# Identity products on TensorE ahead of the first keys, and an earlier place for two norms

## The chip, the cores and the metric

The kernel runs on one core of a Trainium2 chip. A time is the device time of one execution in microseconds (us); the time of the kernel is the median of several executions. Engines are named as the profile names them: PE is TensorE (PEld its weight loads), DVE is VectorE, ACT is ScalarE, POOL is GpSimd, SP is SyncE, which issues most of the DMAs.

## The reference

Two layers. The first is a linear attention with a complex decay, for 4 sequences of 768 steps, 8 heads of 48:

```python
mag = np.sqrt(a_re * a_re + a_im * a_im)
scale = np.minimum(mag, 0.999) / (mag + 1e-06)
a_re_n, a_im_n = (a_re * scale, a_im * scale)
for t in range(S):                       # S = 768
    new_re = ar * S_re - ai * S_im       # ar, ai: the decay of step t
    new_im = ar * S_im + ai * S_re
    kv = np.einsum('bhd,bhe->bhde', k[:, :, t], v[:, :, t])
    S_re, S_im = (new_re + kv, new_im)
    y[:, :, t] = np.einsum('bhd,bhde->bhe', q[:, :, t], S_re)
```

The second takes its 3072 rows of 384 through 8 experts, all of them dense, weighted by a matrix that 8 rounds of row and column scaling make of the gate's logits:

```python
P = np.exp(logits)                       # 3072 x 8
for _ in range(8):
    P /= P.sum(1, keepdims=True) + 1e-09
    P /= P.sum(0, keepdims=True) + 1e-09
    P *= N / E
for e in range(E):                       # E = 8, F = 1024
    out += P[:, e:e + 1] * (np.maximum(x @ w1[e], 0.0) @ w2[e])
```

## The kernel before

The 3072 rows are cut into 12 blocks of 256 (`SUB`), each of two chunks of 128. In the first phase (`phase1`) a block goes through these stations:

- **norm** (`chain`, first half; L450 to L464): the magnitude of the decay is brought to 0.999 at most. ACT squares `z` (the decays) into `sq` (L450), DVE adds (`x`, L455), ACT takes the root twice (`y`, `zz`, L456 to L457), DVE and ACT refine it (L458 to L462), and DVE scales `z` (L464). Blocks 0 to 2 (`NHALF` = 3) do this in two halves, one for each chunk; later blocks in one piece of 768 columns.
- **scan** (`scan`, `cmul`; L368 to L373): DVE forms the running complex products of the decays along a chunk in many small operations on `z` with the temporaries `cm_a` and `cm_b`.
- **keys and queries** (`chain`, second half; L472 to L487): from the products ACT and DVE make the scaled keys `kh` (L485) and, in place of `z`, the scaled queries (L487). The last operation on the queries of block i, half n, is kept as `zl[i, n]`, the second root on ACT (L478) as `sqs[i, n]`. For blocks in one piece n is 0.
- **mix** (`mix`): DMAs spread `kh` into `ks` (SP's queue) and `z` into `qs` (POOL's queue), L510. PE transposes the keys (`ktp`, L531), which ACT copies (`kt`, L533), forms the scores (`sp`, L548), which DVE masks into `sc` (L551), the new state (`U`, L541), which DVE adds up (L602 to L613), and the outputs (`y`, L565). ACT and DVE split them into a rounded part `xh` (L617) and the rest `xl` (L618).
- **experts 0 and 1** (`experts`): 16 steps for a block, 8 for each expert. A step is nine products of `xh` and `xl` with a piece of the first weights (`ph`, L215), two passes on ACT (`hh`, `hf`, L227 and L228), the rest `hl` on DVE (L229), and, up to three steps later (`LAG`), the products with the second weights (`po`, L188 to L190). A block's steps stand between the pieces of the next block's mix.

The second phase takes the other six experts through products that share sums; it is PE's work from end to end and holds most of the time.

Ahead of the mix of block 0, PE also splits the weights. A weight is needed as a rounded part and a rest; `load_w` and `thirds` make the rest on PE, as the identity times the raw weight less the identity times the rounded part (`wd`, L138 and L139 for whole pieces, L164 and L165 for thirds), and ACT copies it out of PSUM (L143, L167). There are two PSUM buffers for each of the two kinds of `wd`, so a piece on PE waits for a copy on ACT. The copies of expert 1 are put behind `g1`, the second root of block 0's second half, on ACT.

The order of the work is set in two ways. PE runs in the order in which the program is written (a manual schedule). For DVE, ACT, POOL and SP a list scheduler orders the instructions by a time line that it works out itself when the program is built. `tc.issue_after(x)` tells it not to put an instruction ahead of `x`. In `chain` this holds the norm of a block behind an operation of the block before:

```python
prev = {2: (1, NCH - 1), 3: (2, NCH - 1), 4: (3, 0)}.get(i)
```

ACT's first square is behind `sqs[prev]`, DVE's first operation behind `zl[prev]`. For blocks 0 to 2 there are fixed orders on DVE and ACT besides. Line numbers are those of the kernel before.

Of the kernel before, what the change touches and what calls it, by code (L numbers as in the profile page):

```python
# [6 lines left out]
F32 = mybir.dt.float32  # L7
# [8 lines left out]
NCT = C // 128  # L16
E, F = 8, 1024
NF = F // 128
CH = 128
SUB = 256  # L20
NCH = SUB // CH
# [2 lines left out]
N1 = 8  # L24
RING = 12
LAG = 3
NHALF = 3
LEAD = {1: 12, 2: 10, 3: 9, 4: 7, 5: 5}
TR = 4
# [6 lines left out]
HEAD = 3  # L36
# [25 lines left out]
class Net:  # L62
# [63 lines left out]
    def load_w(self, e, f, wx, late=None, pool=False):  # L126
        nc = self.nc
        t = self.wt[e, f] = self.wp.tile([128, 2, 2 * C], F32R, tag="w", name=f"w{e}_{f}")
        raw = wx.tile([128, 2 * C], F32, tag="w", name=f"wr{e}_{f}")
        self.wl = nc.sync.dma_start(raw, self.w[e, f])  # L130
        if not pool:
            nc.scalar.activation(t[:, 0, :], raw, AF.Copy)
        else:
            nc.gpsimd.tensor_copy(t[:, 0, :], raw)
        for j in range(2):
            cs = slice(j * C, j * C + C)
            d = (self.psB if j else self.psA).tile([128, C], F32, tag="po" if j else "ph", name=f"wd{e}_{f}_{j}")
            nc.tensor.matmul(d, self.ident, raw[:, cs], start=True, stop=False)  # L138
            nc.tensor.matmul(d, self.nident, t[:, 0, cs], start=False, stop=True)  # L139
            with ExitStack() as st:  # L140
                if late is not None:
                    st.enter_context(self.tc.issue_after(late.ins))
                self.ev.append(nc.scalar.activation(t[:, 1, cs], d, AF.Copy))  # L143

    def thirds(self, e, fs, wx, late):
        nc = self.nc
# [2 lines left out]
        def one(t, f, j):  # L149
# [4 lines left out]
            self.nthird += 1  # L154
            mid = HEAD <= n < 2 * (LAG + 1)
            if not mid:
# [20 lines left out]
    def experts(self):  # L177
# [18 lines left out]
        while True:  # L196
            i, e, f = yield
            if i is None:
                for _ in range(len(pend) if e is None else min(e, len(pend))):
                    l2(*pend.pop(0))  # L200
                continue
            if len(pend) == LAG:
                l2(*pend.pop(0))
# [28 lines left out]
    def phase1(self, c1, ca):  # L232
        tc, nc = self.tc, self.nc
        PS = bass.MemoryType.PSUM
        self.hp = c1.enter_context(tc.tile_pool(name="hp1", bufs=LAG + 1))
        wx = c1.enter_context(tc.tile_pool(name="wx", bufs=NF + N1 - RING))
# [31 lines left out]
        for f in range(NF):  # L268
            self.load_w(0, f, wx)
        g1 = self.sqs[0, 1]  # L270
        for f in range(RING - NF):
            self.load_w(1, f, wx, g1 if f else None, f >= 2)
        loads, splits = self.thirds(1, range(RING - NF, NF), wx, g1)
        for _ in range(2 * (LAG + 1)):
            with tc.issue_after(self.wl.ins):
                loads.pop(0)()
        for _ in range(HEAD):
            splits.pop(0)()

        for i in range(ns):  # L280
            mix = self.mix(i)
            if i == 0:
                n = 0
# [31 lines left out]
            if i == 1:  # L315
                q, z = [self.sqs[1, n] for n in range(NCH)], [self.zl[1, n] for n in range(NCH)]
                x, k = self.dve[1, 0][2], self.dve[1, 0][4]
# [118 lines left out]
    def chain(self, i, parts, zt, qk, alloc):  # L436
        tc, nc = self.tc, self.nc
        V = nc.vector
        fl, ns = self.fl, self.N // SUB
        base = 2 * ns + ns * NCT * NCH  # L440
        z = zt[:, :, :, :CH]
        sq, x, y0, zz = alloc("sq"), alloc("x"), alloc("y0"), alloc("zz")
        prev = {2: (1, NCH - 1), 3: (2, NCH - 1), 4: (3, 0)}.get(i)
        for n in parts or [None]:
            f0, f1 = (base + i, base + NHALF + i) if n else (i, ns + i)
            sq_, x_, y_, zz_, z_ = (t if n is None else half(t, n) for t in (sq, x, y0, zz, z))
            with ExitStack() as st:
                if prev:
                    st.enter_context(tc.issue_after(self.sqs[prev].ins))
                act = self.act[i, n or 0] = [nc.scalar.activation(sq_, z_, AF.Square, accum_out=fl[:, f0:f0 + 1])]  # L450
            ops = self.dve[i, f"n{n or 0}"] = []
            with ExitStack() as st:
                if prev:
                    st.enter_context(tc.issue_after(self.zl[prev].ins))
                ops.append(V.scalar_tensor_tensor(x_, sq_[:, 0], 1e-20, sq_[:, 1], ALU.max, ALU.add))  # L455
            act.append(nc.scalar.activation(y_, x_, AF.Abs_reciprocal_sqrt))  # L456
            act.append(nc.scalar.activation(zz_, y_, AF.Square, accum_out=fl[:, f1:f1 + 1]))  # L457
            ops.append(V.tensor_tensor(x_, x_, zz_, ALU.mult))  # L458
            ops.append(V.scalar_tensor_tensor(y_, x_, -3.0, y_, ALU.add, ALU.mult))
            act.append(nc.scalar.activation(zz_, y_, AF.Square, bias=self.bm05, scale=-0.5e-6))  # L460
            ops.append(V.tensor_scalar(x_, y_, -0.4995, 1.0, ALU.mult, ALU.min))
            ops.append(V.scalar_tensor_tensor(x_, zz_, 0.75, x_, ALU.add, ALU.mult))  # L462
            for a in range(2):
                ops.append(V.tensor_tensor(z_[:, a], z_[:, a], x_, ALU.mult))  # L464
        self.dve["c"] = []
        self.scan(z, alloc)
        for j in range(CH, ZW):
            nc.scalar.activation(zt[:, :, :, j:j + 1], z[:, :, :, CH - 1:CH], AF.Copy)
        sq, x, g0, kh = alloc("sq"), alloc("x"), alloc("g0"), alloc("kh")
        for n in parts or [None]:  # L470
            sq_, x_, g_, z_, qk_, kh_ = (t if n is None else half(t, n) for t in (sq, x, g0, z, qk, kh))
            act = nc.scalar.activation(sq_, z_, AF.Square)  # L472
            self.post.setdefault(i, []).append(act)
            self.dve[i, f"x{n or 0}"] = [V.scalar_tensor_tensor(x_, sq_[:, 0], 1e-26, sq_[:, 1], ALU.max, ALU.add)]
            o = 2 * ns + i * NCT * NCH + (n or 0) * NCT
            self.root[i, n or 0] = [nc.scalar.activation(g_, x_, AF.Abs_reciprocal_sqrt)]
            nc.scalar.activation(fl[:, o:o + x_.shape[1]], x_[:, :, CH - 1], AF.Copy)
            act = nc.scalar.activation(g_, g_, AF.Square)  # L478
            self.root[i, n or 0].append(act)
            ops = self.dve[i, n or 0] = []  # L480
            ops.append(V.tensor_tensor(x_, x_, g_, ALU.mult))
            ops.append(V.scalar_tensor_tensor(g_, x_, -2.0, g_, ALU.add, ALU.mult))
            ops.append(V.scalar_tensor_tensor(x_, g_, -1.0, qk_[:, 1], ALU.mult, ALU.mult))
            for a in range(2):
                ops.append(V.tensor_tensor(kh_[:, a], x_, z_[:, a], ALU.mult))  # L485
            for a in range(2):
                ops.append(V.tensor_tensor(z_[:, a], z_[:, a], qk_[:, 0], ALU.mult))  # L487
            self.sqs[i, n or 0], self.zl[i, n or 0] = act, ops[-1]
# [629 lines left out]
```

## Time and profile before

| what | value |
|---|---|
| time, median of 3 runs (lowest to highest) | 1834.02 us (1833.99 to 1835.79) |
| the profiled execution: its own time, its span | 1835.63 us, 1833.5 us |
| PE busy | 1774.4 us, 97% |
| DVE busy | 1362.3 us, 74% |
| ACT busy | 730.1 us, 40% |
| mean granted TensorE clock | 0.990 |
| instructions | 30712 |

Busy time is the time in which an engine has at least one instruction under way. The granted clock is the share of its full clock that PE was given. A table of stretches has a row for each stretch of the span: its length, the busy time and number of instructions of PE, PEld, DVE, ACT and POOL, the granted clock, the busy share of the DMA engines, and GB/s. A table of waits says which engine at which line waited for which, for how long in all, how often, and the longest. The chain that ended last follows the work back from the last instruction to what released it, step by step.

### The profile page before, as it was taken

The numbers are of one execution on the slowest core, as the hardware profiler recorded it, in microseconds if no ns is written. First come the engines' busy times: TensorE is split into PE (matmuls) and PEld (weight loads), VectorE is DVE, ScalarE is ACT, GpSimd is POOL, SyncE is SP. The second block draws the span as 40 slices with busy tenths as digits, with TensorE's granted clock in tenths as the row PEclk, the third lists the DMA queues.
The fourth block names the chain that finished last, engine by engine and source line by source line (L and its number), as shares of the span: only waits on it lengthen the run. The fifth ranks groups of instructions, "written<-read, shape, count | busy, mean of one in ns | idle before, by whom it ended". The sixth has DMA issues, their size and how long they took to land.

```text
span 1833.5 us, 30712 instructions
## 1 busy us (share of the span) xinstructions
PE 1774.4 (97%) x12024; PEld 1731.9 (94%) x12024; DVE 1362.3 (74%) x3038; ACT 730.1 (40%) x1607; POOL 89.6 (5%) x168
## 2 busy tenths in 40 slices
PE   6989889999999999999999999999999999999998
PEld 3989889999999999899999999998999999999998
DVE  8788899988883587967576767686776767675754
ACT  7444444554543443424243324243433334242421
POOL 3001111111120000000000000000000000000000
PEclk9899999999999999999999999999999999999999
DMA  7344344433332430402010101222220101020100
GB/s 220 94 105 116 81 113 116 123 113 108 117 107 67 147 113 26 147 1 70 1 53 17 52 18 53 65 94 84 85 72 18 53 18 52 1 70 1 52 27 28
DMA packets 104505, 132.84 MB, mean 72 GB/s; under 512 B 9632, under 2 KB 82080, under 8 KB 104352
## 3 DMA queue, kind: packets, MB, share of 16 engines
q1 hardware_dynamic: 98944, 120.89, 21.6%
q0 software_dynamic: 4608, 9.52, 2.1%
q8 instruction: 96, 1.57, 0.4%
q14 instruction: 57, 0.47, 0.1%
q10 hardware_dynamic: 800, 0.39, 0.1%
HBM read 88.22 MB, written 23.59 MB: 61 GB/s over the span
## 4 chain that ended last, share of the span: by engine, by line
PE 80%; DVE 13%; DMA 4%; issue 2%; ACT 1%; SPq 1%; POOL 0%; DVEq 0%
PE po L843 10%; PE po L842 10%; PE po L841 10%; PE P L880 9%; PE P L882 9%; PE P L881 9%; PE ph L215 8%; PE po L188 3%; PE po L190 3%; PE po L189 3%; PE sp L548 2%; PE y L565 2%; DMA raw<-in_w_dram 1%; PE U L541 1%; DVE cm_a L368 1%
## 5 line engine op out<-in xcount | busy, mean ns | idle before, releaser
L843 PE MATMUL po<-wc,hl 128*128 128x384 f32 x1152 | 385.9, 335 | 3.0 <-DVE hl L902 3.0
L841 PE MATMUL po<-wc,hh 128*128 128x384 f32 x1152 | 385.5, 335 | 0.1
L842 PE MATMUL po<-wc,hh 128*128 128x384 f32 x1152 | 385.4, 335 | 0.0
L901 ACT ACTIVATE hh<-c 128x384 fp32r<-128x384 f32 x384 | 200.9, 524 | 322.3 <-DVE c L890 320.9
L902 DVE SCALAR_TENSOR_TENSOR hl<-c,hh 128x384 fp32r<-128x384 f32 x384 | 211.8, 552 | 65.8 <-ACT hh L901 58.0
L215 PE MATMUL ph<-xh,w 128*128 128x256 f32 x1152 | 228.3, 284 | 1.4 <-ACT xh L617 1.4
L843 PEld LDWEIGHTS po<-wc,hl 128*128 128x128 f32 x1152 | 216.4, 188 | 4.4 <-DVE hl L902 4.2
L841 PEld LDWEIGHTS po<-wc,hh 128*128 128x128 f32 x1152 | 216.3, 188 | 0.4 <-ACT hh L901 0.4
L842 PEld LDWEIGHTS po<-wc,hh 128*128 128x128 f32 x1152 | 216.4, 188 | 0.0
L895 ACT ACTIVATE s<-P 128x384 f32<-128x384 f32 x192 | 94.1, 490 | 274.5 <-PE P L882 274.4
L215 PEld LDWEIGHTS ph<-xh,w 128*128 128x128 f32 x1152 | 187.6, 191 | 2.7 <-ACT xh L617 2.3
L227 ACT ACTIVATE hh<-ph 128x256 fp32r<-128x256 f32 x192 | 73.3, 382 | 234.7 <-PE ph L215 234.4
L880 PE MATMUL P<-B,wa 128*128 128x384 f32 x480 | 160.8, 335 | 1.0 <-DVE c L890 0.5
L882 PE MATMUL P<-B,wa 128*128 128x384 f32 x480 | 160.6, 335 | 0.0
L881 PE MATMUL P<-B,wa 128*128 128x384 f32 x480 | 160.5, 334 | 0.0
L215 PE MATMUL ph<-xl,w 128*128 128x256 f32 x576 | 155.0, 283 | 0.5 <-DVE xl L618 0.5
L188 PE MATMUL po<-w,hh 128*128 128x384 f32 x384 | 141.5, 369 | 0.8 <-ACT yst L193 0.8
L190 PE MATMUL po<-w,hl 128*128 128x384 f32 x384 | 131.4, 342 | 3.5 <-DVE hl L229 3.5
L189 PE MATMUL po<-w,hh 128*128 128x384 f32 x384 | 130.5, 340 | 0.0
L890 DVE TENSOR_TENSOR c<-P,u 128x384 f32<-128x384 f32 x192 | 106.1, 553 | 31.3 <-PE P L882 29.3
L890 DVE TENSOR_TENSOR u<-u,s 128x384 f32<-128x384 f32 x96 | 53.3, 555 | 101.0 <-ACT s L895 100.9
L229 DVE TENSOR_TENSOR hl<-hf,hh 128x256 fp32r<-128x256 f32 x192 | 80.0, 419 | 54.4 <-ACT hf L228 52.6
(173 smaller groups left out, 3521.0 us busy)
## 6 DMA issues: line engine op xcount, KB each, us to landing
raw<-in_w_dram SPq DMA_DIRECT2D x48, 768.0 KB, 4.3
qs<-z POOLq DMA_DIRECT2D x144, 64.5 KB, 3.8
qk<-in_aqk_dram SPq DMA_DIRECT2D x12, 768.0 KB, 6.0
ks<-kh SPq DMA_DIRECT2D x144, 64.0 KB, 2.7
ye_d<-yst SPq DMA_DIRECT2D x48, 192.0 KB, 2.8
y<-ye_d SPq DMA_DIRECT2D x48, 192.0 KB, 2.4
z<-in_aqk_dram SPq DMA_DIRECT2D x11, 768.0 KB, 5.4
B<-x_d SPq DMA_DIRECT2D x40, 192.0 KB, 3.7
```

The source lines that it names most:

```text
L188: nc.tensor.matmul(po[k], hh[:, s], w2h, start=f == 0, stop=False)
L189: nc.tensor.matmul(po[k], hh[:, s], w2l, start=False, stop=False)
L190: nc.tensor.matmul(po[k], hl[:, s], w2h, start=False, stop=f == NF - 1)
L215: nc.tensor.matmul(ph, w[:, k, ct * 128:ct * 128 + 128], x[:, ct, :], start=q == 0, stop=q == len(terms) - 1)
L841: nc.tensor.matmul(po[k], hh[:, s], w2[:, 0, i], start=first, stop=False)
L842: nc.tensor.matmul(po[k], hh[:, s], w2[:, 1, i], start=False, stop=False)
L843: nc.tensor.matmul(po[k], hl[:, s], w2[:, 0, i], start=False, stop=last)
L880: nc.tensor.matmul(ps, t[:, 0, k], x[:, 0], start=first, stop=False)
L881: nc.tensor.matmul(ps, t[:, 0, k], x[:, 1], start=False, stop=False)
L882: nc.tensor.matmul(ps, t[:, 1, k], x[:, 0], start=False, stop=last)
L901: A.activation(hh, c, AF.Relu)
L902: V.scalar_tensor_tensor(hl, c, 0.0, hh.bitcast(F32), ALU.max, ALU.subtract)
```

## The change

It has two parts. The first adds 19 products of the 128x128 identity with itself on PE, written into a PSUM tile that nothing reads: 8 ahead of the last whole weight piece of expert 1, 2 each ahead of the second and third of the first three thirds, 7 ahead of the first keys. The second changes what the norms of blocks 3 and 4 are held behind: on DVE, block 3's norm now behind the queries of the first half of block 2 and no longer of the second; on ACT its first square stays where it was held; block 4's norm is held behind nothing of block 3.

```diff
+WARM = (8, 2, 7)
...
+    def warm(self, n):
+        t = self.psY.tile([128, NCT, CH], F32, tag="y", name=f"warm{self.nwarm}")
+        self.nwarm += 1
+        for _ in range(n):
+            self.nc.tensor.matmul(t[:, 0, :], self.ident, self.ident, start=True, stop=True)
...
+        self.nwarm = 0
         for f in range(RING - NF):
+            if f == RING - NF - 1:
+                self.warm(WARM[0])
             self.load_w(1, f, wx, g1 if f else None, f >= 2)
...
-        for _ in range(HEAD):
+        for k in range(HEAD):
+            if k:
+                self.warm(WARM[1])
             splits.pop(0)()
+        self.warm(WARM[2])
...
-        prev = {2: (1, NCH - 1), 3: (2, NCH - 1), 4: (3, 0)}.get(i)
+        prev = {2: (1, NCH - 1), 3: (2, NCH - 1)}.get(i)
...
                 if prev:
-                    st.enter_context(tc.issue_after(self.zl[prev].ins))
+                    st.enter_context(tc.issue_after(self.zl[prev[0], 3 - i if i > 2 else 1].ins))
```

In the changed kernel the lines stand 1 to 13 further down. PE's order differs by the 19 products alone; POOL's is the same. On DVE and ACT the orders are the same until the end of block 2's keys, and differ from there to the end of the first phase and in a few places behind it; SP's differs in 16 places.

The first place is PE ahead of the first keys, `wd1_f_j` being piece or third j of weight f of expert 1. Before:

```order
L138 MATMUL wd1_2_1_467<-wr1_2_460,ident_70 128x384
L139 MATMUL wd1_2_1_467<-w1_2_459,nident_72 128x384
L138 MATMUL wd1_3_0_475<-wr1_3_472,ident_70 128x384
L139 MATMUL wd1_3_0_475<-w1_3_471,nident_72 128x384
L138 MATMUL wd1_3_1_479<-wr1_3_472,ident_70 128x384
L139 MATMUL wd1_3_1_479<-w1_3_471,nident_72 128x384
L164 MATMUL wd1_4_0_506<-wr1_4_0_487,ident_70 128x256
L165 MATMUL wd1_4_0_506<-w1_4_483,nident_72 128x256
L164 MATMUL wd1_4_1_510<-wr1_4_1_490,ident_70 128x256
L165 MATMUL wd1_4_1_510<-w1_4_483,nident_72 128x256
```

And now:

```order
L150 MATMUL warm0_471<-ident_70 128x128 x8
L139 MATMUL wd1_3_0_484<-wr1_3_481,ident_70 128x384
L140 MATMUL wd1_3_0_484<-w1_3_480,nident_72 128x384
L139 MATMUL wd1_3_1_488<-wr1_3_481,ident_70 128x384
L140 MATMUL wd1_3_1_488<-w1_3_480,nident_72 128x384
L171 MATMUL wd1_4_0_515<-wr1_4_0_496,ident_70 128x256
L172 MATMUL wd1_4_0_515<-w1_4_492,nident_72 128x256
L150 MATMUL warm1_519<-ident_70 128x128 x2
L171 MATMUL wd1_4_1_522<-wr1_4_1_499,ident_70 128x256
L172 MATMUL wd1_4_1_522<-w1_4_492,nident_72 128x256
L150 MATMUL warm2_526<-ident_70 128x128 x2
L171 MATMUL wd1_4_2_529<-wr1_4_2_502,ident_70 128x256
```

The products stand between the splits; the last 7 follow the last row's third, and behind them come the keys.

The second place is DVE at the end of block 2's keys and queries (`kh2`, `z2`), with the norm of block 3 (`x3`, `y03`, `z3`), the rests of block 1's steps (`hl1_1_n`: expert 1, block 1, step n) and the first mask of block 2 (`sc0`). Before:

```order
L485 TENSOR_TENSOR kh2_1559<-x2_1557,z2_1447 128x3x128 x2
L487 TENSOR_TENSOR z2_1447<-z2_1447,qk2_1448 128x3x128
L229 TENSOR_TENSOR hl1_1_0_1774<-hf1_1_0_1775,hh1_1_0_1773 128x256
L487 TENSOR_TENSOR z2_1447<-z2_1447,qk2_1448 128x3x128
L455 SCALAR_TENSOR_TENSOR x3_2128<-sq3_2127 128x768
L229 TENSOR_TENSOR hl1_1_1_1796<-hf1_1_1_1797,hh1_1_1_1795 128x256
L229 TENSOR_TENSOR hl1_1_2_1824<-hf1_1_2_1825,hh1_1_2_1823 128x256
L551 COPY_PREDICATED sc0_179<-mask_74,sp2_0_0_1852 128x512
L458 TENSOR_TENSOR x3_2128<-x3_2128,zz3_2130 128x768
L459 SCALAR_TENSOR_TENSOR y03_2129<-x3_2128,y03_2129 128x768
L229 TENSOR_TENSOR hl1_1_3_1877<-hf1_1_3_1878,hh1_1_3_1876 128x256
L461 TENSOR_SCALAR x3_2128<-y03_2129 128x768
```

And now:

```order
L498 TENSOR_TENSOR kh2_1582<-x2_1580,z2_1470 128x3x128 x2
L471 TENSOR_TENSOR x3_2151<-x3_2151,zz3_2153 128x768
L500 TENSOR_TENSOR z2_1470<-z2_1470,qk2_1471 128x3x128
L236 TENSOR_TENSOR hl1_1_0_1797<-hf1_1_0_1798,hh1_1_0_1796 128x256
L500 TENSOR_TENSOR z2_1470<-z2_1470,qk2_1471 128x3x128
L472 SCALAR_TENSOR_TENSOR y03_2152<-x3_2151,y03_2152 128x768
L236 TENSOR_TENSOR hl1_1_1_1819<-hf1_1_1_1820,hh1_1_1_1818 128x256
L236 TENSOR_TENSOR hl1_1_2_1847<-hf1_1_2_1848,hh1_1_2_1846 128x256
L474 TENSOR_SCALAR x3_2151<-y03_2152 128x768
L564 COPY_PREDICATED sc0_179<-mask_74,sp2_0_0_1875 128x512
L475 SCALAR_TENSOR_TENSOR x3_2151<-zz3_2153,x3_2151 128x768
L477 TENSOR_TENSOR z3_2144<-z3_2144,x3_2151 128x6x128 x2
```

Block 3's first norm operation now stands a few rows ahead of these, its second and third have moved ahead of the second half of block 2's queries and of `hl1_1_1`, and its last ones ahead of `hl1_1_3`.

The third place is ACT at block 3's keys (`sq3`, `g03`) and block 4's first square (`sq4`, held behind block 3's second root before), with the two passes of block 2's steps (`hh0_2_n`, `hf0_2_n`). Before:

```order
L472 ACTIVATE sq3_2219<-z3_2121 128x1536
L227 ACTIVATE hh0_2_3_2310<-ph0_2_3_2300 128x256
L228 ACTIVATE hf0_2_3_2312<-ph0_2_3_2300 128x256
L647 ACTIVATE P_90<-lt2_2316 128x16
L227 ACTIVATE hh0_2_4_2336<-ph0_2_4_2326 128x256
L476 ACTIVATE g03_2221<-x3_2220 128x768
L477 ACTIVATE fl_91<-x3_2220 128x6
L228 ACTIVATE hf0_2_4_2338<-ph0_2_4_2326 128x256
L478 ACTIVATE g03_2221<-g03_2221 128x768
L450 ACTIVATE sq4_2792,fl_91<-z4_2786 128x1536
```

And now:

```order
L485 ACTIVATE sq3_2242<-z3_2144 128x1536
L234 ACTIVATE hh0_2_0_2275<-ph0_2_0_2258 128x256
L235 ACTIVATE hf0_2_0_2277<-ph0_2_0_2258 128x256
L234 ACTIVATE hh0_2_1_2284<-ph0_2_1_2265 128x256
L235 ACTIVATE hf0_2_1_2286<-ph0_2_1_2265 128x256
L654 ACTIVATE ls2_2297<-lp2_2290 16x256
L489 ACTIVATE g03_2244<-x3_2243 128x768
L490 ACTIVATE fl_91<-x3_2243 128x6
L463 ACTIVATE sq4_2815,fl_91<-z4_2809 128x1536
L234 ACTIVATE hh0_2_2_2309<-ph0_2_2_2299 128x256
L235 ACTIVATE hf0_2_2_2311<-ph0_2_2_2299 128x256
L491 ACTIVATE g03_2244<-g03_2244 128x768
```

Block 3's square stands three steps sooner in block 2's work, and block 4's square has moved between the two roots of block 3.

## The prediction

> **What bounds the kernel now.** I read the times first, then the page's chain that ended last, then a table of stretches, and only then the early rows in order of time. The profiled execution took 1835.6 us, its span 1833.5 and 2.1 around it; the median of the runs is 1834.02, so this execution lies 1.6 above it. 0.2% of it, 3.7 us, is about what a measurement of this kernel can tell from no change.
>
> ```profile
> PE 80%; DVE 13%; DMA 4%; issue 2%; ACT 1%; SPq 1%; POOL 0%; DVEq 0%
> ```
> ```profile
> 29.75:33.16 3.41, 2.95 (x12) 1.65 (x10) 2.50 (x6) 2.08 (x4) 3.41 (x3) 1.00 0.92 304
> 33.16:36.57 3.41, 1.04 (x5) 0.49 (x3) 2.83 (x6) 3.21 (x9) 1.44 (x3) 1.00 0.18 57
> 36.57:39.98 3.41, 3.41 (x9) 2.16 (x8) 3.38 (x8) 3.27 (x9) 1.57 (x3) 0.50 0.29 76
> 39.98:43.40 3.42, 1.47 (x7) 0.81 (x6) 3.35 (x8) 2.42 (x9) 2.44 (x6) 1.00 0.91 169
> 43.40:57.05 13.65, 12.85 (x81) 11.69 (x82) 9.52 (x20) 4.52 (x12) 3.64 (x9) 0.50 0.93 209
> 57.05:60.46 3.41, 3.41 (x35) 3.41 (x34) 1.73 (x5) 2.60 (x9) 0.63 (x1) 1.00 0.00 0
> 125.29:128.70 3.41, 1.58 (x13) 1.26 (x12) 3.35 (x8) 0.97 (x5) 0.00 (x0) 1.00 0.43 173
> 197.00:203.84 6.84, 5.49 (x23) 5.52 (x24) 6.28 (x11) 1.92 (x3) 0.94 (x2) 0.50 0.91 226
> 234.50:237.90 3.40, 2.34 (x17) 2.21 (x17) 3.40 (x6) 1.07 (x2) 0.00 (x0) 1.00 0.00 0
> 265.30:268.70 3.40, 3.40 (x13) 3.40 (x14) 3.34 (x7) 2.42 (x5) 0.00 (x0) 0.50 0.00 0
> 300.00:1833.00 1533.00, 1510.02 (x9862) 1490.47 (x9860) 1104.71 (x2402) 581.63 (x1228) 38.44 (x72) 1.00 0.20 62
> ```
> Columns: stretch, its length, busy us of PE, PEld, DVE, ACT, POOL, granted TensorE clock, DMA share, GB/s. From 300 us on PE is busy 1510 of 1533 us at full clock: whatever reaches it earlier ends the kernel earlier, us for us. So all that can be won lies ahead of 300, in PE's waits and in the stretches at clock 0.50. The other rows show the rule of the clock here. It changes at steps of 3.41 us. A step with PE busy 30%, 43% or 46% (1.04, 1.47, 1.58 of 3.41) is followed by one at 0.50; a step with 69% (234.50) is not. After the second drop the clock stayed at 0.50 for four steps, though PE was busy 12.85 of 13.65 us: what keeps the clock does not bring it back at once.
>
> ```profile
> 32.83 0.63 PE L139 MATMUL wd<-w,nident 128*128 128x384 f32 x1
> ...
> 35.84 0.96 PE L138 MATMUL wd<-wr,ident 128*128 128x384 f32 x2 [2.37 <-ACT w L143]
> ...
> 41.52 0.70 PE L164 MATMUL wd<-wr,ident 128*128 128x256 f32 x2 [0.89 <-ACT w L143]
> ...
> 44.20 1.73 PE L531 MATMUL ktp<-ident,ks 112*128 112x112 f32 x8 [1.86 <-DMA ks<-kh]
> ...
> 56.51 1.20 PE L531 MATMUL ktp<-ident,ks 112*128 112x112 f32 x8
> ```
> ```profile
> 45.93 1.73 PE sp L548 x8
> ...
> 57.70 0.91 PE sp L548 x8
> ```
> ```profile
> DVE sc L551 <- PE sp L548: 3.8, 4, 1.6
> DVE xl L618 <- ACT xh L617: 2.7, 2, 1.5
> ```
> First PE in order of time (start, us, line, tiles, count, in brackets the idle time ahead and what ended it), then the scores in the chain that ended last, then DVE's waits from 44 to 65 us (total, times, longest). PE works without a gap from the first keys (44.20) on, at half clock until 57, and it is DVE that waits for it.
>
> **Part 1, 19 identity products.** They add 8 + 2 + 2 + 7 products of 128x128. The nearest row is the scores, L548: also 128 columns out of 128, 8 records for four products. In the chain those 8 take 1.73 us at half clock and 0.91 at full clock, so one product costs 0.43 or 0.23 us. At full clock the 8 take 1.8 us of the 2.37 ahead of 35.84; 2 of the 4 take 0.46 of the 0.89 ahead of 41.52, the other 2 stand ahead of wd1_4_1, whose split is no longer late; the 7 take 1.6 of the 1.86 ahead of the keys. All are covered by waits for ACT (L143 behind the roots of block 0) and for the keys' DMA, which the change leaves alone; without that cover they would cost 19 x 0.23 = 4.4 us. No engine reads the tiles, so nobody waits for them, and PE's tile y0 comes behind them on PE itself.
>
> What they do to the clock: the step 33.16 to 36.57 gets 1.04 + 1.8 = 2.8 us of work (83%), the next ones keep 69% or more, since at full clock PE then idles about 1.0 us ahead of wd1_4_0, 0.4 ahead of 41.52 and 0.3 ahead of the keys. That is at or above the 69% that held, well above the 46% that did not. Then keys, scores and states run at full clock as they do in the step 57.05 to 60.46, which held it with just this work. The stretch 44.20 to 56.51, 12.3 us at 0.50, shrinks to 0.91/1.73 of itself: 6.5 us, 5.8 less. The other end of the bound is DVE, which can gain no more than the 6.5 us it waits there. Both agree, and I take PE's **-5.8**. DVE's and ACT's order from there on is fixed and all of it moves up; the loads that block 1 and 2 need are behind the same instructions. If the clock is lost in one step after all, half comes back: -2.5 is the small end, -6.5 the large.
>
> The Trainium skill says in "TensorE: Matmul & The Clock Gate", section "Why this matters for your kernels", that idle gaps of PE above some 3 us are to be avoided. By that rule the gaps of 2.37, 0.89 and 1.86 us would have been harmless, and part 1 would be worth 0. The trace disagrees: 0.50 follows them in two places, so as a case of its own (1834 - 5.7, near 1828) I give it no chance beyond that of rival (a), which ends at the same time.
>
> **Part 2, the norms of blocks 3 and 4.** The stage from 140 to 285 us alternates between DVE's chain for the next block and PE.
>
> ```profile
> PE y L565 <- DVE sc L551: 3.0, 3, 2.4
> PE ktp L531 <- issue: 2.9, 1, 2.9
> PE sp L548 <- DMA qs<-z: 2.6, 2, 2.2
> PE po L190 <- DVE hl L229: 1.7, 1, 1.7
> ```
> ```profile
> 148.50 0.42 DVE L229 TENSOR_TENSOR hl<-hf,hh 128x256 fp32r<-128x256 f32 x1 [1.73 <-ACT hf L228]
> ...
> 149.69 0.94 DVE L458 TENSOR_TENSOR x<-x,zz 128x768 f32<-128x768 f32 x1
> ...
> 173.59 0.55 DVE L618 TENSOR_TENSOR xl<-y,xh 128x384 fp32r<-128x384 f32 x1
> ...
> 178.64 0.34 DVE L373 TENSOR_TENSOR z<-cm_a,cm_b 128x186 f32<-128x186 f32 x1
> ...
> 188.03 1.82 DVE L485 TENSOR_TENSOR kh<-x,z 128x768 f32<-128x768 f32 x2
> ...
> 190.10 1.82 DVE L487 TENSOR_TENSOR z<-z,qk 128x768 f32<-128x768 f32 x2
> ...
> 195.16 0.96 DVE L458 TENSOR_TENSOR x<-x,zz 128x768 f32<-128x768 f32 x1 [1.27 <-ACT zz L457]
> ...
> 201.04 0.56 DVE L368 TENSOR_TENSOR cm_a<-z 128x384 f32<-128x384 f32 x1
> ...
> 228.08 0.96 DVE L455 SCALAR_TENSOR_TENSOR x<-sq 128x768 f32<-128x768 f32 x1 [2.48 <-ACT sq L450]
> ...
> 237.09 1.82 DVE L485 TENSOR_TENSOR kh<-x,z 128x768 f32<-128x768 f32 x2
> ```
> ```profile
> 184.33 1.49 ACT L450 ACTIVATE sq<-z 128x1536 f32<-128x1536 f32 x1
> ```
> ```profile
> 195.59 0.58 PE L531 MATMUL ktp<-ident,ks 112*128 112x112 f32 x4 [2.85 <-issue]
> 198.35 2.05 PE L548 MATMUL sp<-qs,ks 112*128 112x128 f32 x8 [2.19 <-DMA qs<-z]
> 235.56 0.44 PE L190 MATMUL po<-w,hl 128*128 128x384 f32 x1 [1.67 <-DVE hl L229]
> 264.19 0.43 PE L565 MATMUL y<-sc,v 128*32 128x128 f32 x8 [2.42 <-DVE sc L551]
> ```
> First PE's waits from 185 to 290 us (11.0 in all, these four groups 10.2), then DVE, ACT and PE in order of time. Walking DVE's new order with these durations, in before's time:
>
> Block 3. Its first three norm operations (x3 at L455, L458, L459, 0.95 each) now stand ahead of hl1_1_2, so they fill the 1.73 us ahead of 148.50. Its scan ends about 2.9 us sooner than at 178.98, of which 0.7 is only hl0_2_0 and hl0_2_1 put behind. Against it: ACT now has sq4 (L450, 1.49 at 184.33, 0.2 more for its sum) ahead of the second root of block 3 (L478), and two of block 4's operations (0.95 each) stand ahead of kh3 on DVE, a third ahead of the queries z3. Keys come 1.05 us sooner than 188.03, queries about 0.1 later than 190.10. PE's scores at 198.35 wait for the queries' DMA, so block 3 starts when it did: 0. The small part xl2 (173.59) is now behind four more operations of the scan, about 2 us later, and PE with it by 1.1 to 1.5; PE's waits at 195.59 and 198.35 (5.0) cover that.
>
> Block 4. Its norm no longer waits for block 3's queries; its first three operations and the wait of 1.27 ahead of 195.16 are gone from behind them. Its scan starts at about 196.3 instead of 201.04. Five hl, xl3 and the mask of chunk 1 that stood inside the scan now come later, so it ends some 6.5 us sooner; and the norm of block 5, for which DVE waited 2.48 at 228.08, is squared on ACT sooner too. Keys of block 4 are ready near 228 instead of 238. From then on PE has what it waited for: half of the 1.67 at 235.56, the 2.42 at 264.19 with the step at 0.50 that it causes (3.40 us of PE, 1.6 of them lost by the ratio above), and 1.6 us of small waits (from the other groups of the 11.0 and the rest of y). Sum 0.8 + 2.4 + 1.6 + 1.6 = 6.4; less 0.7 for hl that now come later: **-5.7**. The small end is +1.5 (xl2 late without cover), the large end all 11.0 and half of the three steps at 0.50 (197.00 to 203.84 and 265.30), 16; I stay near the walk, since each of its terms has a row. SP's queue also changes (ks4's copies stand behind the stores of xl3 and two of ye); the 10 us by which those keys are early cover it, so it costs 0, and up to some us of that lead if they don't. z2's load is one weight load later in that queue: 0, covered by DVE's whole scan of block 1 ahead of its use.
>
> **Sum.** 1835.6 - 5.8 - 5.7 = 1824.1 on the profiled execution, 1822.5 on the median. Steps of the clock fall anywhere in a run, so part of the 1.6 between them is in my terms already. I say 1823.5.
>
> **Rivals.** (a) *The products do not hold the clock.* If a transpose counts as idle, the step with the first keys has 0.3 us of wait and 1.0 of keys (56.51 to 57.54) out of 3.41, 62% busy, between 46 and 69; the clock drops at the keys again and part 1 gives 0: 1834 - 5.7, about 1828.5. Against it speaks the step 57.05 with half a us of keys. The Trainium skill says in "TensorE: Matmul & The Clock Gate", section "Part 4: PE-mode transpose", that a transpose does not count as busy in the same way; no row here isolates one. (b) *DVE's lead is spent.* Keys of block 4 earlier change nothing if hl or masks, now behind more scan work, stop PE instead (as at 235.56): part 2 gives 0, 1834 - 5.8, about 1828. For it: the four groups above are all of that kind. (c) *Slower: the products run at half clock.* If 0.50 is granted before or in the first 8, these take 3.4 us instead of 2.4, the four 1.7 instead of 0.9, the 7 3.0 instead of 1.9: the keys start 2.9 to 3.5 us later than 44.20, and the stretch behind stays as long. That alone is 1834 + 3.5, near 1837.5, and it decides as soon as the clock in 36.57 to 43.40 is 0.50 and part 2 gives nothing. Against it: the row 29.75 to 33.16 is work at 86% and full clock, and the 8 follow it without a gap.
>
> **Numbers.** Both parts as worked out 0.60; (a) 0.14; (b) 0.16; (c) 0.05; smaller things of either sign 0.05. The first is 1823.5 with 1819 to 1827 of its own. The range takes in (a) and (b): 1818 to 1830. Faster by over 0.2% (below 1830.3) holds the first three cases but for their tails: 0.85; within 0.2%: 0.10; slower: 0.05.
>
> **What would show it.** Clock 1.00 from 33 to 60 us; 8 scores in about 0.9 us behind the first keys, which still start near 44; the first rows of the experts (L215) some 6 us sooner. Later, by the same shift, PE still waiting some 3 to 5 us for block 3's keys and queries, and no wait of over 1 us from there on. Wrong would be: 0.50 in any step from 36 to 57 (part 1), keys later than 44.5 (c), or PE's waits behind block 3 as large as the four groups above (b).

## The result, and the profile after

The changed kernel takes 1824.38 us (median of 9 runs, 1818.67 to 1829.48) against 1833.73 before (9 runs, 1831.49 to 1835.87): a ratio of 0.9944, 95% interval 0.9929 to 0.9959, or 7.5 to 13 us less. Forecast were 1823.5 us and 1818 to 1830. Two things were not forecast: single executions scatter more than twice as far as before, and the two profiled executions lie 13.6 us apart (1835.63 and 1822.02), more than the medians.

The stretches of the profile after, as shown of before (stretch, its length, busy us of PE, PEld, DVE, ACT, POOL, granted clock, DMA share, GB/s):

```profile
34.12:37.53 3.41, 2.82 (x15) 1.76 (x13) 3.31 (x7) 3.41 (x11) 1.12 (x2) 1.00 0.13 38
37.53:40.95 3.42, 2.26 (x14) 1.97 (x14) 3.32 (x8) 3.21 (x11) 3.11 (x6) 1.00 0.63 148
40.95:44.36 3.41, 2.67 (x20) 2.46 (x21) 3.41 (x9) 1.51 (x5) 2.44 (x6) 1.00 1.14 181
44.36:57.05 12.69, 12.69 (x180) 11.92 (x182) 11.49 (x25) 6.77 (x20) 2.41 (x6) 1.00 0.80 202
88.73:92.16 3.43, 2.09 (x17) 2.12 (x18) 2.54 (x6) 2.82 (x9) 1.62 (x4) 1.00 1.14 211
116.04:119.45 3.41, 1.85 (x15) 1.49 (x13) 3.35 (x8) 1.22 (x5) 0.00 (x0) 1.00 0.45 179
184.31:187.72 3.41, 0.75 (x5) 0.60 (x6) 3.38 (x7) 1.15 (x3) 3.04 (x6) 1.00 1.11 179
187.72:191.13 3.41, 3.41 (x14) 3.41 (x14) 3.27 (x9) 0.49 (x1) 0.00 (x0) 0.50 1.02 296
```

The clock is 1.00 through the first keys; between 30 and 300 us of this execution only one step of 3.41 us is left at half clock (187.72), where before there were ten. PE's rows there and its waits from 185 to 290 us (total, times, longest):

```profile
35.19 0.91 PE L139 MATMUL wd<-wr,ident 128*128 128x384 f32 x2 [0.16 <-ACT w L144]
41.61 1.72 PE L150 MATMUL warm<-ident 128*128 128x128 f32 x14
44.06 0.96 PE L544 MATMUL ktp<-ident,ks 112*128 112x112 f32 x8 [0.73 <-DMA ks<-kh]
50.57 0.93 PE L544 MATMUL ktp<-ident,ks 112*128 112x112 f32 x8
90.07 0.57 PE L544 MATMUL ktp<-ident,ks 112*128 112x112 f32 x4 [2.25 <-DMA ks<-kh]
187.55 1.89 PE L561 MATMUL sp<-qs,ks 112*128 112x128 f32 x8 [2.62 <-DMA qs<-z]
```
```profile
PE sp L561 <- DMA qs<-z: 2.6, 1, 2.6
PE ph L222 <- DVE xl L631: 1.7, 1, 1.7
PE po L197 <- DVE hl L236: 0.8, 1, 0.8
PE U L554 <- ACT kt L546: 0.2, 1, 0.2
```

Of 11.0 us of waits in this stage 5.3 are left. The 1.7 for `xl` is a new wait, of block 3's rest at 220.64: `xl` now stands on DVE behind block 4's keys. Since PE's order is the same in both but for the products, each of its 12024 matmuls can be set beside itself. The lead of the changed kernel's PE along the way, from the starts of the same instruction in the two traces:

```
                                     before     after     lead
first keys                            44.20     44.06     -0.14
second keys                           56.51     50.57     -5.94
block 1's first keys                  97.44     90.07     -7.37
a step of the experts                103.79     94.84     -8.94
behind the wait for hl               134.88    124.49    -10.39
behind the waits for xl2 and hf      178.07    169.57     -8.50
block 3's first scores               198.35    187.55    -10.80
block 4's y                          264.19    249.57    -14.62
behind xl of block 4                 285.66    268.41    -17.25
first check of the second phase      628.39    611.34    -17.06
P, second weights                    676.26    661.03    -15.22
behind the next step of the clock    679.14    665.38    -13.76
near the end                        1763.75   1750.51    -13.24
```

### The profile page after: what moved, and what is told of

The parts are those of the page before. It is cut to its first block, busy times and chain, and to the rows that moved or that the text cites. A ratio compares the mean times of both kernels' runs of the same rounds, so it can differ in the third digit from the quotient of the medians.

```text
span 1819.5 us, 30778 instructions
## 1 busy us (share of the span) xinstructions
PE 1768.3 (97%) x12062; PEld 1726.9 (95%) x12062; DVE 1360.0 (75%) x3038; ACT 730.1 (40%) x1607; POOL 89.4 (5%) x168
## 4 chain that ended last, share of the span: by engine, by line
PE 81%; DVE 11%; DMA 3%; ACT 2%; issue 1%; SPq 1%; DVEq 0%; ACTq 0%
PE po L856 10%; PE po L854 10%; PE po L855 10%; PE P L893 9%; PE P L894 9%; PE P L895 9%; PE ph L222 9%; PE po L195 3%; PE po L197 3%; PE po L196 3%; PE sp L561 2%; PE y L578 2%; DMA raw<-in_w_dram 1%; PE U L554 1%; DVE c L903 1%
```

## The experiments

Each ratio is against the kernel before, timed on the same chip beside it; in us it is that share of 1833. "Mean clock" is the mean granted clock over a kernel's executions; before it is 0.9909 (15 executions), with the change 0.9958. "Lead" is again how much sooner PE starts an instruction in a trace than in the trace of before.

The number of products also enters the time line of the list scheduler, so some of these kernels have another order on DVE and ACT than the changed kernel. By the order of the instructions in the traces, the two versions with transposes have the same one; the norms alone, the first 12 products and the first version with two more gaps differ in at most 5 instructions, all behind 190 us. The last 7 alone and the doubled products differ most: some 470 of DVE's 3038 instructions stand elsewhere, from 98 us on. Ahead of that DVE and ACT run in the same order in all of them; the whole times of these two can't be put down to the products alone.

**One part at a time.** The products alone:

```diff
-        prev = {2: (1, NCH - 1), 3: (2, NCH - 1)}.get(i)
+        prev = {2: (1, NCH - 1), 3: (2, NCH - 1), 4: (3, 0)}.get(i)
...
-                    st.enter_context(tc.issue_after(self.zl[prev[0], 3 - i if i > 2 else 1].ins))
+                    st.enter_context(tc.issue_after(self.zl[prev].ins))
```

> The 19 products alone; the norms of blocks 3 and 4 are held as before. My theory (clock held from 36 to 57 us, and nothing else): 12.3 us at half clock become 6.5, so 1833.7 - 5.8 = 1828 and a ratio of 0.9968, the first rows of the experts 5.8 to 6.2 us sooner, and PE's waits of 2.9, 2.2 and 2.4 us for block 3's keys and queries and block 4's mask still there. Rival A (the products also spare the steps at half clock at 98 and 129 us, as in the changed kernel's trace, where PE was 10.4 us ahead at 140 us): 1823 to 1825, ratio 0.994 to 0.995. Rival B (the products gain in few executions, the steps of the clock fall anywhere): a ratio of 0.998 or more, and times that scatter by over 5 us.

Measured: 1824.29 us, 0.9960 (0.9948 to 0.9972), -7.3 us, mean clock 0.9948.

```profile
85.35:88.77 3.42, 2.69 (x20) 2.48 (x19) 3.25 (x8) 1.24 (x4) 2.46 (x6) 1.00 0.91 230
88.77:92.18 3.41, 1.92 (x16) 1.95 (x17) 2.34 (x5) 2.80 (x9) 1.82 (x4) 1.00 1.15 188
```
```profile
186.34 0.57 PE L544 MATMUL ktp<-ident,ks 112*128 112x112 f32 x4 [3.80 <-issue]
188.25 2.05 PE L561 MATMUL sp<-qs,ks 112*128 112x128 f32 x8 [1.34 <-DMA qs<-z]
213.48 0.42 PE L578 MATMUL y<-sc,v 128*32 128x128 f32 x8 [1.67 <-DVE sc L564]
```

The waits of blocks 3 and 4 stay, as expected of both theories. The time lies between them: 5.8 is inside the interval, but the trace is rival A's; rival B (0.998 or more) is out. PE's lead is 5.7 at the second keys and 10.2 at block 1's last steps (134.88 before; 10.4 in the changed kernel): the wait for block 1's keys is 2.23 us in place of 3.42 and parted by a step's edge, so that 56% is the least busy step there, and the clock is kept. From 206 us on some 100 of DVE's instructions stand in another order than before; the lead grows from 10.1 to 11.3 there, so in this trace 1.2 us at most come from it.

The norms alone (the kernel before with the two lines of part 2):

> The norms of blocks 3 and 4 moved, without any product. My theory: -5.7 by the walk, -6.9 by the shift of PE between 140 and 300 us in the two traces, so 1827 to 1828, ratio 0.9965; the half clock at the first keys is back (8 scores in 1.7 us), and PE's waits for block 4's keys and masks are gone. Rival (b) (DVE's lead is spent on what is put behind the scan): 0, 1834. Rival C (the two parts need one another: without the earlier start DVE is the later one everywhere): -2 or less, 1832.

Measured: 1827.21 us, 0.9967 (0.9954 to 0.9980), -6.0 us, mean clock 0.9918. My -5.7 holds; (b), with 0, is out, and C, with -2, too. The half clock at the keys is back (41.05 to 47.88 in its trace).

Block 4's norm alone, and block 3's alone:

```diff
-        prev = {2: (1, NCH - 1), 3: (2, NCH - 1), 4: (3, 0)}.get(i)
+        prev = {2: (1, NCH - 1), 3: (2, NCH - 1)}.get(i)
```
```diff
-                    st.enter_context(tc.issue_after(self.zl[prev].ins))
+                    st.enter_context(tc.issue_after(self.zl[(2, 0) if i == 3 else prev].ins))
```

> Block 4's norm alone is held behind nothing of block 3; block 3's norm waits for both halves of block 2's queries as before, and there are no products. My walk gave the move of block 3 a worth of 0 and all of -5.7 to block 4: as the run of both norms, 1828, ratio 0.9969. Rival D (block 3's move is worth the wait for block 3's keys, 2.9 us at 195.59): 1830 to 1831, ratio 0.9985. Rival E (block 4's norm alone makes block 3's keys late, since three of its operations stand ahead of them on DVE): 1834 or more, with PE's wait for block 3's keys grown from 2.9 to 5 us.

> Block 3's norm alone is held behind the first half of block 2's queries; block 4's norm is held behind block 3's queries as before, and there are no products. My walk: 0, 1834, ratio 1.000, since block 3 starts when its queries have landed and these come no sooner. Rival D: block 3's keys and queries come up to 2.9 us sooner, PE's waits at 195.59 and 198.35 (5.0 us) shrink to 2, so 1831, ratio 0.9984. Rival E: the small part of block 2 comes late and PE waits for it ahead of block 3: 1835 or more.

Measured: block 4's alone 1826.15 us, 0.9963 (0.9950 to 0.9976), -6.8; block 3's alone 1829.35 us, 0.9978 (0.9968 to 0.9988), -4.0. The first is what my walk gave, the second is not. PE at block 3's keys and scores, with block 4's norm alone:

```profile
195.91 0.57 PE L531 MATMUL ktp<-ident,ks 112*128 112x112 f32 x4 [4.44 <-DMA ks<-kh]
200.38 2.05 PE L548 MATMUL sp<-qs,ks 112*128 112x128 f32 x8 [3.89 <-DMA qs<-z]
```

and DVE's keys and queries of block 3 with block 3's norm alone, then PE there:

```profile
185.49 1.83 DVE L485 TENSOR_TENSOR kh<-x,z 128x768 f32<-128x768 f32 x2
187.57 1.82 DVE L487 TENSOR_TENSOR z<-z,qk 128x768 f32<-128x768 f32 x2
```
```profile
196.04 0.55 PE L531 MATMUL ktp<-ident,ks 112*128 112x112 f32 x4
196.43 1.07 PE L548 MATMUL sp<-qs,ks 112*128 112x128 f32 x8
...
220.77 0.43 PE L565 MATMUL y<-sc,v 128*32 128x128 f32 x8 [3.06 <-DVE sc L551]
```

Rival E's mechanism is there in the first (the keys' wait grew from 2.85 to 4.44), though not its time of 1834 or more, and rival D's in the second (keys and queries 2.5 us sooner, both waits gone, 0.9984 inside the interval). I read it so: block 4's operations cost block 3's queries what block 3's earlier norm gives them, and so the two together are worth no more than block 4's alone (-6.0 and -6.8, which can't be told apart). Of the -4.0 of block 3's move its own trace shows little: that execution was the slowest of its ten, and its lead at 300 us is 0.3. Where the others win it stays open.

**Which products hold the clock.** The changed kernel with WARM = (8, 2, 0), and with (0, 0, 7):

> The changed kernel with the first 12 products only (8, 2 and 2); the 7 ahead of the first keys are left out. By the steps of all six traces so far, a step of 3.41 us with PE busy under about half of it is followed by half clock, one with more is not. The clock then holds at 36.6, but the step with the wait for the first keys has a gap of 2.5 us or more again (1.7 of products + 0.7 that is left now) and falls below half in most executions: half clock at the keys for two to four steps, 3 to 6 us lost, 1827 to 1830, as with the norms alone (ratio 0.9965 to 0.998). Rival F (the first drop is what brings the second, the 12 are enough): as the changed kernel, 1824, ratio 0.9944. Rival G (it needs a whole gap of over 3 us): 1824 too, and no half clock at all before 85 us.

> The changed kernel with the last 7 products only, ahead of the first keys; the first 12 are left out. By the share of the step: the wait of 2.3 us ahead of 35.8 still costs one step at half clock (36.6 to 40), which lies ahead of waits and costs nothing, and the last 7 fill the step ahead of the keys, so keys, scores and states run at full clock: as the changed kernel, 1824 to 1825, ratio 0.9945. Where the steps fall so that the half clock of the first wait still stands at 41 us, it reaches into the keys: some executions 3 to 6 us slower. Rival H (a clock once dropped stays low over the small products of the keys, whatever fills the gap): 1828 to 1830, ratio 0.998.

Measured: the first 12 give 1827.72 us, 0.9973 (0.9964 to 0.9982); the last 7 give 1821.33 us, 0.9941 (0.9927 to 0.9955), which can't be told from all 19. H falls, and F and G by the median (1824 was their time). Without the last 7 the times part in two groups: four of 11 lie from 1821.8 to 1824.2 with a clock of 0.994 to 0.996, seven from 1826.2 to 1830.0 with 0.991 to 0.994. The execution that was traced is of the first group, with two steps just at half, which kept the clock:

```profile
39.94:43.35 3.41, 1.72 (x10) 1.17 (x8) 3.34 (x8) 2.41 (x9) 2.44 (x6) 1.00 0.94 180
43.35:46.76 3.41, 1.78 (x18) 1.81 (x18) 3.41 (x9) 2.28 (x6) 2.44 (x5) 1.00 1.18 177
46.76:57.00 10.24, 10.24 (x133) 9.47 (x135) 9.39 (x19) 5.25 (x16) 1.50 (x4) 1.00 0.82 223
```

No execution of the second group was traced, so that these lose the clock at the keys is argued from their clock and time, not seen. With the last 7 alone the first step drops as before and is over when the keys come:

```profile
33.38:36.80 3.42, 0.92 (x4) 0.42 (x3) 2.87 (x5) 3.02 (x10) 1.84 (x4) 1.00 0.32 106
36.80:40.21 3.41, 3.41 (x9) 2.20 (x7) 3.38 (x8) 3.27 (x8) 1.17 (x3) 0.50 0.16 40
40.21:43.62 3.41, 2.39 (x16) 1.98 (x16) 3.31 (x8) 2.82 (x10) 2.43 (x5) 1.00 0.92 192
43.62:57.00 13.38, 13.09 (x158) 12.13 (x160) 13.25 (x29) 7.41 (x21) 3.95 (x9) 1.00 0.95 218
88.00:91.41 3.41, 0.72 (x7) 0.51 (x5) 2.20 (x5) 2.54 (x8) 3.13 (x6) 1.00 0.91 197
91.41:98.23 6.82, 5.93 (x26) 5.96 (x27) 5.71 (x13) 1.55 (x3) 0.00 (x1) 0.50 0.83 184
```

Its wait for block 1's keys is 3.58 us. That wait is 2.2 to 2.6 us in all six traces with the first products in place (transposes and doubled ones among them, and nothing ahead of these keys) and 3.4 to 4.0 in the five without. So the last 7 are enough to hold the clock at the first keys, and the shorter wait at block 1's goes with the first 12; by which way was not tried.

**Products or transposes.** The same 19 made as transposes of the identity, and twice as many:

```diff
-            self.nc.tensor.matmul(t[:, 0, :], self.ident, self.ident, start=True, stop=True)
+            self.nc.tensor.transpose(t[:, 0, :], self.ident, self.ident)
```

> The changed kernel with the 19 products made as transposes of the identity on PE (same tile, same count, about the same time each) in place of ordinary products. If a transpose counts as work for the clock as its time on PE does: as the changed kernel, 1824, ratio 0.9944, clock 1.00 from 33 to 57 us. Rival (a) of the prediction (a transpose counts as idle): the half clock at 36.6 and at the keys is back, 1828 to 1830, ratio 0.997 to 0.998.

> The 19 products made as 38 transposes of the identity (16, 4, 4 and 14). One transpose took half as long as one product (7 in 0.93 us against 1.72), so this fills the same waits with transposes for the same time; the run with 19 left 2.25 us ahead of the first keys and a step 34% busy. If a transpose counts by its time on PE: clock 1.00 from 33 to 57 us, as the changed kernel, ratio 0.9944. Rival (a) (it counts as idle): half clock at the keys as with 19 of them, ratio 0.998 to 0.999.

Measured: 19 transposes 1831.86 us, 0.9989 (0.9976 to 1.0001); 38 of them 1820.55 us, 0.9940 (0.9927 to 0.9952). The first is even slower than rival (a) said (0.997 to 0.998), and for another reason. One transpose took half as long as one product (0.93 us for 7; the changed kernel's 7 products took 1.72):

```profile
42.02 0.93 PE L150 MATMUL warm<-ident 128*128 128x128 f32 x7
```
```profile
32.63:36.05 3.42, 1.92 (x12) 1.42 (x11) 2.87 (x5) 3.15 (x10) 1.81 (x4) 1.00 0.35 113
36.05:39.46 3.41, 2.52 (x12) 1.69 (x11) 3.37 (x7) 3.27 (x9) 1.21 (x3) 1.00 0.19 46
42.87:46.29 3.42, 1.17 (x12) 1.12 (x12) 3.42 (x9) 1.60 (x4) 2.82 (x6) 1.00 0.85 191
46.29:53.11 6.82, 6.82 (x34) 6.59 (x33) 3.78 (x8) 1.74 (x7) 1.09 (x3) 0.50 0.72 195
```

So they filled half of the wait, and the step with the keys came to 34%. Where they made a step of 56% (32.63, 1.0 of its 1.92 us are transposes), the clock was kept; without them it would be 26%, and no step as empty kept it from 20 us on. With 38 of them it holds as with 19 products:

```profile
42.55:45.96 3.41, 2.38 (x24) 2.17 (x23) 3.41 (x9) 1.79 (x4) 3.21 (x6) 1.00 1.16 156
45.96:57.00 11.04, 11.04 (x138) 10.27 (x140) 10.22 (x21) 6.05 (x19) 1.72 (x5) 1.00 0.87 227
```

So a transpose counted for the clock by its time on PE. The Trainium skill says in "TensorE: Matmul & The Clock Gate", section "Part 4: PE-mode transpose", that a transpose does not count as busy in the same way. These two runs speak against it. Why the 19 transposes came out 4 us slower than the norms alone (0.9989 against 0.9967), which have no products at all, is not explained.

**More products.** The numbers doubled, WARM = (16, 4, 14):

> The changed kernel with every number of products doubled: 16, 4, 4 and 14, another 19. At 0.22 us each they are 4.2 us more. The waits that are left in the changed kernel are 0.16, 0.89, 0.71 and 0.73 us, so the 16 run 1.6 us past the first wait, of which 0.9 come back at the next one, the 4 and 4 fill what is left there, and the 14 take 3.1 us where 2.3 are: the keys start 1 to 2 us later, all else the same, 1825.5 to 1826.5, ratio 0.995 to 0.9955. Rival J (the products' cover is no matter, since DVE has slack there): 1824.4, ratio 0.9944. Rival K (steps fuller still hold the clock in more executions): 1823, ratio 0.9935.

Measured: 1818.79 us (1816.41 to 1819.47), 0.9922 (0.9909 to 0.9935), mean clock 0.9976. I expected slower than the changed kernel and was wrong; the way is rival K's (0.9935), the size is more than it said. The interval still overlaps that of the changed kernel (0.9929 to 0.9959).

```profile
33.00:57.00 24.00, 24.00 (x231) 22.41 (x233) 22.60 (x45) 16.41 (x47) 10.60 (x20) 1.00 0.76 181
```
```profile
45.28 0.93 PE L546 MATMUL ktp<-ident,ks 112*128 112x112 f32 x8
```

The keys do start 1.2 us later (45.28 against 44.06), but PE has no wait at all from 33 to 57 us, and the 1.2 are gone at block 3's scores (187.27 against 187.55): these wait 2.62 us for their queries in the changed kernel and not at all here. Its five executions have a clock of 0.997 or 0.998, those of the changed kernel 0.992 to 0.998, so the worse ones with more half clock are missing. That the fuller steps did it is not shown: DVE's other order came with the same edit, and with it PE's wait for `hl` near 120 us is 0.86 us in place of 1.84. In the two traces the doubled kernel's PE is still 1.2 us behind at 300 us, and ahead only from the half clock of the changed kernel at 662 us on.

More gaps: products ahead of block 1's first keys, and between block 3's first keys and scores, with (9, 10) beside all 19, with (12, 10) beside the last 7 alone, and with (10, 10) beside the doubled ones:

```diff
+            def fill(n, U=U):
+                for _ in range(n):
+                    nc.tensor.matmul(U.rearrange("p h d -> p (h d)")[:, :CH], self.ident[:, :SK], self.ident, start=True, stop=True)
...
+            if (i, c) == (1, 0):
+                fill(FILL[0])
             keys(0)
+            if (i, c) == (3, 0):
+                fill(FILL[1])
```

> The changed kernel with 19 more products: 9 ahead of block 1's first keys (the wait of 2.25 us at 90) and 10 between block 3's first keys and scores (the wait of 2.62 us at 187.6). They take 2.0 and 2.2 us at full clock, inside those waits. By the share of the step they take away the half clock at 188 (1.3 to 1.7 us), the one behind block 1's keys in the executions that have it (0 to 1.7 us, 3 at most), and leave the waits as they are: 1821 to 1823, ratio 0.9925 to 0.9935, and a narrower scatter than 1818.7 to 1829.5. Rival I (the clock of those steps is covered by other waits, or the products push the scores): 1824 to 1826, ratio 0.9944 or above.

> The last 7 products only, with 12 ahead of block 1's first keys (a wait of 3.58 us in the run with the last 7) and 10 between block 3's first keys and scores. By the share of the step: the step of half clock behind block 1's keys, two in that run's trace, goes in nearly all executions (1.5 to 3 us), the one at 188 too where it stands, so 1818 to 1821, ratio 0.992 to 0.9935. Rival I (something else stops PE there instead, as the wait of 1.8 us for ACT at 209 in the run with two more gaps): 1822 to 1824, ratio 0.994 to 0.995.

> The doubled products (16, 4, 4 and 14) together with 10 ahead of block 1's first keys and 10 between block 3's first keys and scores. Both kept the clock in stretches of their own (33 to 57 us; 88 to 99 and 184 to 194 us), and the doubled run's mean clock was 0.9976 already, so there is little left to spare: if they add, 1815 to 1817.5, ratio 0.991 to 0.992, mean clock 0.998 or more. Rival L (the doubled run has no half clock left in the two gaps, its keys being late by more than PE): as the doubled run, 1818.5 to 1819, ratio 0.9922 to 0.9925. Rival I (late scores or ACT behind them): 1820 or more.

Measured: 1822.27 us, 0.9953 (0.9940 to 0.9966); 1816.74 us, 0.9913 (0.9898 to 0.9927); 1820.86 us, 0.9929 (0.9915 to 0.9943). The first is rival I by its ratio (0.9944 or above): both gaps keep the clock, the scatter is 3.7 us, but a wait of 1.80 us for ACT behind block 3's keys is new, with half clock behind it. The second is better than I forecast (0.992 to 0.9935) and the best version here, ahead of the changed kernel, narrowly, by interval against interval (timed on different chips, each against the kernel before). Its orders on DVE and ACT are almost those of the changed kernel (18 and 3 instructions stand elsewhere). In its trace the gap ahead of block 1's keys is a step of 83%:

```profile
88.61:92.02 3.41, 2.82 (x27) 2.65 (x26) 2.20 (x6) 2.54 (x8) 2.58 (x5) 1.00 1.02 193
```

The third adds nothing to the doubled products: the ratio is nearer to rival L, the time is rival I's (1820 or more), and rival I's waits are there (1.60 us for DVE at 205.66 and 2.13 for ACT at 214.16), both with the clock kept. So these gains did not add. Since the order on DVE differs between the two as well (some 500 instructions), and the same two gaps gave 2.8 thousandths to the last 7 and nothing to all 19, what the gaps are worth by themselves stays open.

## Why the prediction was right, point by point

**Part 1, -5.8.** The lead between first and second keys is 5.80 us in the traces: the mechanism and the size at that place are as worked out. The step that failed is that the sum stopped at 57 us, as if the clock stayed as it was from there on: the drops at 98 and 129 us went too, and block 1's keys came 1.2 us nearer. Alone the part measured -7.3, and PE's lead at 135 us is 10.2. The bound of 6.5 from DVE's waits covered the first keys only.

**The rule of the clock.** I had 46% that drops and 69% that holds. In the 14 traces, from 20 to 1800 us, there are 37 steps at full clock with PE busy under 47% of 3.41 us, all followed by half clock; of those from 47 to 61%, 31 kept it and 11 did not; of over 7000 at 61% or more none lost it. So the step's share decides, but for a band from 47 to 61% in which these traces don't show what does. The length of one gap does not: 2.25 us parted by an edge (90.07) keeps the clock, 1.83 that lie whole within a step (ahead of 128.66 before) lose it. The clearest case is that last wait, of 1.83 or 1.84 us for `hl`, which stands in eleven of the traces: in six it lies within one step and the clock is lost, in five a step's edge parts it and the clock is kept. By the Trainium skill ("TensorE: Matmul & The Clock Gate", section "Why this matters for your kernels") gaps above some 3 us are what to avoid; here shorter ones did most of the harm, in every trace: of the 48 drops 39 had no gap above 3 us.

**Rival (a)** fell: ordinary products held the clock, and so do transposes of enough time. **Rival (c)** fell: the first 8 ran at full clock and the keys start at 44.06.

**Part 2, -5.7**, measured alone -6.0. Where DVE's walk can be compared, it holds almost to the digit. Moved by the lead of 10.4 us at 140 us, the keys of block 3 start at 186.87 (forecast 186.98), its queries end at 191.97 (191.92 before, "0.1 later"), the keys of block 4 start at 226.96 and end at 228.79 ("ready near 228"):

```profile
176.47 1.82 DVE L498 TENSOR_TENSOR kh<-x,z 128x768 f32<-128x768 f32 x2
...
180.62 0.95 DVE L500 TENSOR_TENSOR z<-z,qk 128x768 f32<-128x768 f32 x1
...
216.56 1.83 DVE L498 TENSOR_TENSOR kh<-x,z 128x768 f32<-128x768 f32 x2
```

PE loses 1.9 us of its lead at 165 (forecast 1.1 to 1.5, all by the late xl2): 0.3 of it is PE's wait for xl2, and 0.9 a wait for `hf` on ACT that the walk did not have; the rest is in smaller pieces. The waits at block 3 covered it: the lead at block 3's scores is 10.80, 0.4 from where it was. From there to 285 us it grows by 6.4, where the terms gave 5.7. That is after a loss that the walk did not have:

```profile
220.64 0.98 PE L222 MATMUL ph<-xl,w 128*128 128x256 f32 x6 [1.73 <-DVE xl L631]
```

No wait of over 1 us was to come behind block 3's queries, and this one did. It is rival (b)'s mechanism in one place: block 3's `xl`, which now stands behind more of block 4's work on DVE, stops PE. The lead falls from 11.9 to 10.1 there, and the terms of block 4 bring back more than that. What I read wrong is the worth of block 3's move by itself: 0 is its worth beside block 4's, not alone. Rival (b) as a whole fell, since part 2 did not come to 0.

**Us for us from 300 us on** is where the traces lose 4 of 17. At the change to the second phase PE waits for DVE in both. In the trace of the changed kernel these waits (0.42 and 1.23 us) fell into one step:

```profile
658.76:662.17 3.41, 1.76 (x10) 1.44 (x9) 2.77 (x8) 1.27 (x3) 0.00 (x0) 1.00 0.00 0
662.17:665.59 3.42, 3.42 (x13) 3.42 (x12) 2.29 (x8) 0.75 (x2) 0.00 (x0) 0.50 0.00 0
```

The lead went from 17.06 to 15.22 in the waits up to there, which are longer than before, and to 13.76 in the step at half clock. The trace of before has a step of 54% at that place and kept its clock, so this is a cost that either kernel can have.

**The sum.** The terms add to -11.5, the forecast took -10.5 of the median, and the medians differ by 9.4. Two misses partly cancelled: part 1 was worth more than its term, and the parts together less than apart (-7.3 and -6.0 against -10.3, though with intervals 4 to 6 us wide). That both mechanisms are there is shown; that the time came within 1 us is in part luck. Why the parts don't add is not settled.

## What to carry to other kernels

Look at the granted clock step by step, not at its mean: find each step of 3.41 us in which the matrix engine is busy less than about 60% and fill the wait in it with products that nobody reads. One trace is not enough to find them: a wait that an edge parts in this execution lies within a step in another, so look at every wait, or pair of close waits, of more than about 1.3 us (39% of a step). Filling past the end of the wait did no harm at the first keys here, a fill that fell short lost the clock. A filler pays only as far as its gain is kept through the next waits, and more fillers did not always pay more. The edit can also move the scheduler's order on other engines; compare the orders before a time is put down to the filler. Parts of a reordering should be costed together: here each of the two norms alone was worth at least two thirds of the pair.

## What had not been expected

The edges of the steps lie at another place in every trace, so a wait of about half a step brings half clock in one and nothing in the next. The changed kernel's scatter of 10.8 us probably comes from there: its slowest execution (1829.48 us) has a mean clock of 0.992, the two fastest 0.997 and 0.998. Only one of its executions was traced, so this is not shown. With the doubled products it was 3.1 us (5 runs). How long half clock lasts varies as well. Of 48 stretches 32 lasted one step, 12 two, one three and three four: at the first keys it was left after two steps (41.05 to 47.88 with the norms alone) or after four (43.40 to 57.05 before), with PE busy all of the last one or three; what ends it was not found. And 56% and 60% busy lost the clock once each, at 208 us behind a wait for ACT in the runs with 22 and 19 products in the two gaps, where other steps as full kept it.
